# Attention feeding a spectral mix on one core: two pairs' row sums moved to the vector engine, one weight block split elsewhere, and a reordered vector queue in every sixth slot

## The chip, the cores and the metric

The kernel runs on one core of one Trainium2 chip. The metric is the device time of one execution in microseconds. Three runs of the kernel before took 980.04, 981.16 and 984.58 us; the median, 981.16, is what the changed kernel is compared with.

## What is computed

Attention with 8 batches, 12 heads, 448 positions and 64 channels per head, with scores capped by tanh, and behind it a mixing layer over the 768 channels that the heads make together:

```python
scores = scale * np.matmul(q, k.transpose(0, 1, 3, 2))
scores = cap * np.tanh(scores / cap)
scores = scores - np.max(scores, axis=-1, keepdims=True)
attn = np.exp(scores)
attn = attn / (np.sum(attn, axis=-1, keepdims=True) + 1e-09)
x = np.matmul(attn, v)              # then (batch, 448, 768)
theta = x @ w_theta
zr, zi = x * np.cos(theta), x * np.sin(theta)
y = einsum('ts,bsd->btd', w_tok_r, zr) + einsum('ts,bsd->btd', w_tok_i, zi)
u = x + y
out = u + np.maximum(u @ w_ch, 0.0)
```

All arrays are float32. Where the cap is at most 64 the kernel leaves out the subtraction of the maximum; that is the arm that runs here.

## The kernel before

**The unit of work is a pair of heads**, 48 in all (8 batches of 6 pairs), one pair `k` per slot `s`. A slot forms the scores of pair `s` in two halves (`qk_half`, L193), and on ScalarE tanh (L195) and exp (L201, `exp_half`) of each half; for the pair of the slot before it forms the product with v (`av`, L233; ScalarE copies it out, L236) and the row sums. Slots 0 to 7 are the start, in which the weights are loaded and split too. From slot 8 on every slot also carries one sixth of the mixing layer of one batch: slot `8 + 6b + part`, with `part` 0 to 5 and a script of its own for each part (`part_scripts`, L359). There are 56 slots.

**Row sums.** `sums` (L250) multiplies a matrix of ones with the exponentials and leaves them in a PSUM tile `r` for two pairs. Pairs below `DIRECT` feed their four chunks to TensorE (`sum_pair`, L239: 8 matmuls for a pair; the trace shows two records for each). The pairs from `DIRECT` on are first added up on VectorE to a tile `ps` (`add_half`, L215: one add at L223, two at L226), and both pairs of a sum go to TensorE together, with 2 matmuls each. `invert` (L265) takes the reciprocal of `r` on VectorE and sends it by four DMAs (L279) to the tiles `bc`; `norm` (L281) multiplies by them later.

**Matmuls of reduced precision in two parts.** The weights and, in the mixing layer, the data are split into a high and a low part. A weight block is loaded (`load`, L95), scaled (`scale`, L100, on ScalarE) and split (`split`, L103) by six or seven operations on VectorE: L106 to L109, then the cast to the high part, on ScalarE (L111) for `w_ch` and on VectorE (L113) for the others, then L114 and L115 for the low part. Where the cast is on ScalarE, ScalarE waits for L107, and VectorE for the cast. The blocks are called th0 to th5 (`w_theta`), ch0 to ch5 (`w_ch`) and tk0 to tk6 (`w_tok`). th and ch blocks are loaded into the two buffers `g_sb`, even ones into the first and odd ones into the second, which the mixing layer uses as well; tk blocks go through the buffers of the tiles `zh` and `zl`.

**When a weight step is done** stands in the table `WEIGHTS` (L142): for slot and place in it (`a`, `b`, `c`) a list of steps, `>x` for load, `*x` for scale, `x` for split. From pair 14 (`WHOLE`) on q and k are split as well: `prep` (L174) makes the tiles `hi` and `lo` of the next pair on VectorE (L178, L179) and issues the next load of q, k. DMAs are all issued from SP's queue, in the program's order, and a DMA that waits for its buffer holds up those behind it.

**The mixing layer of a batch.** Parts 0 and 1: six projections `th` (`theta`, L306; L299 to L301), brought to the range of the sine by ScalarE (L310, L311) and VectorE (L312 to L314); sines and cosines on ScalarE (`sincos`, three blocks at a time); `rotate` (L321) multiplies them with x on VectorE. From part 1's end to part 3: `transp` (L325) transposes a block on TensorE in two PSUM tiles of 4 and 3 pieces; for each ScalarE makes the high part `zh` (L333) and VectorE the low part `zl` (L334); `mix` (L337) multiplies them with the tk weights, and VectorE adds the result to x (L344). Parts 4 and 5: six projections `ch` (`chan`, L346), their result (L352) and the output.

**PSUM.** The scores take one tile in psS. All else, the results `a`, `r`, `th`, `t`, `mx` and `ch`, comes from one pool, psM, with four buffers. A new tile takes a buffer whose readers stand ahead of it in the program, the one that is freed first there, and its first matmul waits for that reader.

The engines run their own queues in the order in which the program is written; nothing is reordered.

Of the kernel before, what the change touches and what calls it, by code (L numbers as in the profile page):

```python
# [25 lines left out]

FIRST = 8

DIRECT = 10

WHOLE = 14

# [2 lines left out]
def softcap_attn_then_spectral_mix(ctx, tc, qk2, v, cap, w_theta, w_tok, w_ch, ident, outT):  # L35
    nc = tc.nc
# [7 lines left out]
    NS = B * NP  # L44
# [7 lines left out]
    w_theta, w_ch = (w.bitcast(I32).rearrange("m p j (n two) -> m p j n two", two=2) for w in (w_theta, w_ch))  # L52
# [16 lines left out]
    wch_h = const.tile([P, NJ, DM], F32R, name="wch_h")  # L69
    wch_l = const.tile([P, NJ, DM], F32R, name="wch_l")  # L70
# [14 lines left out]
    class Split:  # L85
# [14 lines left out]
        def scale(self):  # L100
            nc.scalar.activation(self.hw, self.hw, AF.Copy, scale=2.0**-112)

        def split(self):  # L103
            t, hi, lo, hw, lw = self.t, self.hi, self.lo, self.hw, self.lw
            ti = t.bitcast(I32)
            nc.vector.tensor_scalar(ti, hw.bitcast(I32), 3, None, op0=ALU.logical_shift_left)  # L106
            nc.vector.scalar_tensor_tensor(ti, hw.bitcast(I32), -(2**31), ti, op0=ALU.bitwise_and, op1=ALU.bitwise_or)  # L107
            nc.vector.tensor_scalar(hw.bitcast(I32), ti, -(2**23), None, op0=ALU.bitwise_and)
            nc.vector.scalar_tensor_tensor(lw, lw.bitcast(U32), 2.0**-52, hw, op0=ALU.mult, op1=ALU.mult)  # L109
            if self.act:  # L110
                nc.scalar.copy(hi, t)  # L111
            else:
                nc.vector.tensor_copy(hi, t)  # L113
            nc.vector.tensor_tensor(t, t, hi.bitcast(F32), op=ALU.subtract)  # L114
            nc.vector.tensor_tensor(lo, t, lw, op=ALU.add)  # L115

    def room_g(i):
        def room():
            st = g_sb[i % 2].rearrange("p x y s -> p (x y s)")
            raw = st[:, : 2 * DM].rearrange("p (j n two) -> p j n two", j=NJ, two=2)  # L120
            return raw, st[:, 2 * DM : 3 * DM].rearrange("p (j n) -> p j n", j=NJ)
        return room
# [8 lines left out]
    steps = {}  # L131

    def weight_steps():
        for m in range(NJ):
            ms = slice(m * P, (m + 1) * P)
            steps["th", m] = Split(room_g(m), w_theta[m], wth_h[:, :, ms], wth_l[:, :, ms])
            steps["ch", m] = Split(room_g(m), w_ch[m], wch_h[:, :, ms], wch_l[:, :, ms], True)
        for c in range(NC2):
            steps["tk", c] = Split(room_z(S, f"swk{c}"), w_tok[c], wtk_h[:, c], wtk_l[:, c])

# [7 lines left out]
    }  # L148

    def weights(s, pos):  # L150
        for word in WEIGHTS.get((s, pos), "").split():
            step = steps[word[-3:-1], int(word[-1])]
            {">": step.load, "*": step.scale}.get(word[0], step.split)()


    hi, lo, vt, pt, pst, bc = {}, {}, {}, {}, {}, {}
# [17 lines left out]
    def prep(k):  # L174

        hi[k] = wk.tile([P, 2, S], F32R, tag="hi", name=f"hi{k}", bufs=1)
        lo[k] = wk.tile([P, 2, S], F32R, tag="lo", name=f"lo{k}", bufs=1)
        nc.vector.tensor_copy(hi[k], raw[k])  # L178
        nc.vector.tensor_tensor(lo[k], raw[k], hi[k].bitcast(F32), op=ALU.subtract)  # L179
        if k + 1 < NS:  # L180
            load_qk(k + 1)
# [83 lines left out]
    def invert(k):  # L265

        if k % 2 == 0:
            return
        r = state.pop("r")
        ri = wk.tile([P, S], F32, tag="ri", name=f"ri{k}", bufs=1)  # L270
        if state["general"]:
            nc.vector.tensor_scalar_add(ri, r[:, :S], 1e-9)
            nc.vector.reciprocal(ri, ri)
        else:
            nc.vector.reciprocal(ri, r[:, :S])  # L275
        for n in (k - 1, k):
            bc[n] = wk.tile([P, S], F32, tag="bc", name=f"bc{n}", bufs=2)
            for i in range(2):
                nc.sync.dma_start(bc[n][i::2, :], ri[D * (n % 2) : D * (n % 2) + D, :])  # L279
# [90 lines left out]
    def us(b, j):  # L370
        split_x(b, j, "us")

    def pipeline(general):
        state["general"] = general
        load_v(0)
        load_qk(1)
        for step in (("tk", 0), ("tk", 1)):
            steps[step].load()

        for s in range(FIRST + 6 * B):  # L380
            k = s - 1
            b, part = divmod(s - FIRST, 6)
            live = s < NS
            start = s < FIRST
            if live:
                qk_half(s, 0)
            if start:
                weights(s, "a")
                exp_half(s, 0)
            if 0 <= k < NS:  # L390
                av(k)
            if not start:
                weights(s, "a")
            if not start and part == 4:
                for j in range(NJ // 2, NJ):
                    us(b, j)
            if s + 1 < NS:
                load_v(s + 1)
            if 0 <= k < NS:
                sums(k, (0,) if start else (0, 1))  # L400
                if not start:
                    invert(k)
            if live:
                qk_half(s, 1)
            if 0 <= k and start:
                sums(k, (1,))
            if s + 2 <= WHOLE:
                load_qk(s + 2)
            if WHOLE <= s + 1 < NS:
                prep(s + 1)  # L410
            weights(s, "b")
            if 0 <= k and start:
                invert(k)
            script = ["B", "a", "b"] if start else part_scripts(b)[part]
            for i, e in enumerate(script):
                if not start and i == len(script) - 1:
                    weights(s, "c")
                    if s % 2 == 1 and s <= NS + 1:
                        norm(s - 3)
                        norm(s - 2)  # L420
                if isinstance(e, str):
                    if live:
                        if e in "AB":
                            exp_half(s, "AB".index(e))
                        else:
                            add_half(s, "ab".index(e))
                else:
                    e[0](b, e[1])
            if start:
                weights(s, "c")  # L430
                for n in {4: (0, 1), 5: (2, 3), 7: (4, 5)}.get(s, ()):
                    norm(n)
                for j in {6: range(4), 7: range(4, NJ)}.get(s, ()):
                    split_x(0, j, "xs")
# [52 lines left out]
```

## Time and profile before

| | |
|---|---|
| median of 3 runs | 981.16 us (980.04 to 984.58) |
| profiled execution, its own time | 981.55 us |
| its span, first to last instruction | 979.7 us |
| granted clock of TensorE, mean of the span | 0.995 |
| TensorE busy | 953.9 us (97%) |
| VectorE busy | 631.6 us (64%) |
| ScalarE busy | 597.4 us (61%) |
| DMA queue of the program | 22.7% of 16 engines' span |

Busy times are of one profiled execution; 1.85 us of its time lie around the span. Times in the rows further on are microseconds from the span's start. On TensorE's timeline slot 9 begins at 107.9, slot 10 at 129.5, slot 11 at 154.5, slot 12 at 175.6, slot 13 at 194.2, and slot 16, the part 2 of batch 1, runs from 252.5 to 275.8. A matmul's duration in the profile overlaps that of its neighbours, so the cost of a train of matmuls is read from its start to the start of the next one. The granted clock is 1.00 at 2.4 GHz; 0.5 would be 1.2 GHz throughout.

### The profile page before, as it was taken

The page shows a single profiled execution, that of the slowest core. Times are in us where ns is not written, and L with a number is a line of the kernel's source. Part 1 is how long each engine was busy: PE and PEld are TensorE (multiplying, and loading weights), DVE is VectorE, ACT ScalarE, POOL GpSimd, SP SyncE. Part 2 cuts the span into 40 slices and gives each one's busy share as a digit, 9 for nine tenths or more (in the row PEclk, how much of TensorE's full clock was granted, in tenths as well). Part 3 has the DMA queues.
Part 4 walks back from the last instruction along what each step waited for, and adds up shares of the span by engine and source line. Part 5 has one row for each costly group of instructions (what it writes and reads, how often), then busy time and mean ns, then how long its engine had stood idle before and what let it go on. Part 6 is the DMA issues. An engine that isn't in the chain of part 4 may idle for free.

```text
span 979.7 us, 12717 instructions
## 1 busy us (share of the span) xinstructions
PE 953.9 (97%) x5192; PEld 693.5 (71%) x5192; DVE 631.6 (64%) x865; ACT 597.4 (61%) x615; POOL 0.4 (0%) x6
## 2 busy tenths in 40 slices
PE   6999999989999999999999999999999999999997
PEld 2333667657787787777677767876877777789897
DVE  5788665885865658557676567665586566763541
ACT  5887676466954677555876469636784567642520
POOL 0000000000000000000000000000000000000000
PEclk9999999999999999999999999999999999999999
DMA  6654221322102211032111321122211330102001
GB/s 221 196 186 127 66 69 39 121 98 85 48 29 76 79 54 48 30 104 76 38 48 36 106 67 46 49 68 75 66 48 29 86 93 29 29 1 76 1 1 60
DMA packets 30739, 68.68 MB, mean 70 GB/s; under 512 B 4304, under 2 KB 16720, under 8 KB 30672
## 3 DMA queue, kind: packets, MB, share of 16 engines
q1 hardware_dynamic: 30672, 67.78, 22.7%
q8 instruction: 43, 0.70, 0.3%
q14 instruction: 24, 0.20, 0.1%
HBM read 45.74 MB, written 11.01 MB: 58 GB/s over the span
## 4 chain that ended last, share of the span: by engine, by line
PE 78%; DVE 10%; ACT 9%; DMA 2%; issue 1%; SPq 0%; DVEq 0%
PE a L233 13%; PE s L193 12%; PE mx L341 6%; PE mx L342 6%; PE mx L343 6%; PE ch L299 6%; PE ch L301 6%; PE ch L300 6%; PE th L299 4%; PE th L300 4%; PE th L301 4%; PE r L248 3%; ACT p L195 3%; PE t L332 3%; DVE ri L275 2%; ACT p L201 1%
## 5 line engine op out<-in xcount | busy, mean ns | idle before, releaser
L195 ACT ACTIVATE p<-s,qscale 112x1792 f32<-112x1792 f32 x96 | 168.7, 1757 | 171.2 <-PE s L193 171.1
L201 ACT ACTIVATE p<-p,cap_sb 112x1792 f32<-112x1792 f32 x96 | 170.6, 1790 | 0.5
L233 PE MATMUL a<-p,v 112*64 112x448 f32 x768 | 155.5, 547 | 0.0
L341 PE MATMUL mx<-wtk_h,zh 128*128 128x448 f32 x336 | 126.3, 376 | 1.8 <-DVE zl L334 1.8
L342 PE MATMUL mx<-wtk_l,zh 128*128 128x448 f32 x336 | 122.9, 366 | 0.0
L343 PE MATMUL mx<-wtk_h,zl 128*128 128x448 f32 x336 | 122.9, 366 | 0.0
L233 PEld LDWEIGHTS a<-p,v 112*64 112x64 f32 x768 | 51.0, 137 | 87.9 <-issue 78.5
L299 PE MATMUL ch<-us,wch_h 128*128 128x448 f32 x288 | 107.2, 372 | 0.0
L299 PE MATMUL th<-xs,wth_h 128*128 128x448 f32 x288 | 106.9, 371 | 0.0
L301 PE MATMUL ch<-us,wch_l 128*128 128x448 f32 x288 | 105.6, 367 | 0.0
L300 PE MATMUL ch<-us,wch_h 128*128 128x448 f32 x288 | 105.5, 366 | 0.0
L300 PE MATMUL th<-xs,wth_h 128*128 128x448 f32 x288 | 105.4, 366 | 0.0
L301 PE MATMUL th<-xs,wth_l 128*128 128x448 f32 x288 | 105.3, 366 | 0.0
L226 DVE TENSOR_TENSOR ps<-ps,p 112x896 f32<-112x896 f32 x76 | 82.7, 1088 | 1.3
L275 DVE RECIPROCAL ri<-r 128x448 f32<-128x448 f32 x24 | 70.9, 2954 | 14.8 <-PE r L248 14.8
L312 DVE SCALAR_TENSOR_TENSOR g_sb<-g_sb 128x448 f32<-128x448 f32 x48 | 30.0, 624 | 72.6 <-ACT g_sb L311 72.2
L334 DVE TENSOR_TENSOR zl<-t,zh 128x512 fp32r<-128x512 f32 x96 | 55.2, 617 | 24.9 <-ACT zh L333 24.9
L341 PEld LDWEIGHTS mx<-wtk_h,zh 128*128 128x128 f32 x336 | 63.2, 188 | 7.7 <-DVE zl L334 3.0
L352 DVE SCALAR_TENSOR_TENSOR x<-ch,x 128x448 f32<-128x448 f32 x48 | 29.8, 621 | 59.0 <-PE ch L301 59.0
L343 PEld LDWEIGHTS mx<-wtk_h,zl 128*128 128x128 f32 x336 | 63.1, 188 | 5.3
L342 PEld LDWEIGHTS mx<-wtk_l,zh 128*128 128x128 f32 x336 | 63.2, 188 | 4.8
L344 DVE TENSOR_TENSOR x<-mx,x 128x448 f32<-128x448 f32 x48 | 29.9, 623 | 52.9 <-PE mx L343 52.3
(71 smaller groups left out, 1411.6 us busy)
## 6 DMA issues: line engine op xcount, KB each, us to landing
qk_sb<-in_qk SPq DMA_DIRECT2D x35, 448.0 KB, 3.3
v<-in_v SPq DMA_DIRECT2D x48, 224.0 KB, 2.5
bc<-ri SPq DMA_DIRECT2D x96, 112.0 KB, 2.3
out_dram<-x SPq DMA_DIRECT2D x48, 224.0 KB, 2.0
qk<-in_qk SPq DMA_DIRECT2D x13, 448.0 KB, 3.3
g_sb<-in_wth SPq DMA_DIRECT2D x6, 768.0 KB, 5.1
g_sb<-in_wch SPq DMA_DIRECT2D x6, 768.0 KB, 5.3
swk_raw<-in_wtok SPq DMA_DIRECT2D x7, 448.0 KB, 4.2
```

The lines of the kernel that those rows point to most:

```text
L193: nc.tensor.matmul(sp[:CP, i, hh, :S], kk[k][rows, 1, ks], qq[k][rows, 0, :], start=n == 0, stop=n == len(products) - 1)
L195: nc.scalar.activation(pp, sp[:CP, :, :, :S], AF.Tanh, scale=qscale[:CP])
L201: nc.scalar.activation(pp, pp, AF.Exp, scale=cap_sb[:CP])
L226: nc.vector.tensor_tensor(pst[k], pst[k], pt[k, 1][:, i], op=ALU.add)
L233: nc.tensor.matmul(acc[hh * D : (hh + 1) * D, :S], va[:, hh, c, :], pt[k, c // 2][:, c % 2, hh, :], start=c == 0, stop=c == NCH - 1)
L275: nc.vector.reciprocal(ri, r[:, :S])
L299: nc.tensor.matmul(acc[:, :S], wh[:, j, ms], t[:, 0, :], start=j == 0, stop=False)
L300: nc.tensor.matmul(acc[:, :S], wh[:, j, ms], t[:, 1, :], start=False, stop=False)
L301: nc.tensor.matmul(acc[:, :S], wl[:, j, ms], t[:, 0, :], start=False, stop=j == NJ - 1)
L341: nc.tensor.matmul(acc[:, :S], zh[:, c, :], wtk_h[:, c, :], start=c == 0, stop=False)
L342: nc.tensor.matmul(acc[:, :S], zh[:, c, :], wtk_l[:, c, :], start=False, stop=False)
L343: nc.tensor.matmul(acc[:, :S], zl[:, c, :], wtk_h[:, c, :], start=False, stop=c == NC2 - 1)
```

## The change

- Pairs 8 and 9 are no longer direct: their exponentials are added on VectorE in slots 8 and 9, and their row sums go to TensorE together in slot 10.
- The split of tk6 moves from the end of slot 8 to the start of slot 9, ahead of that of ch1.
- Block ch2 is scaled on VectorE (`vscale`) and cast to its high part on VectorE, at the start of slot 11, where it was scaled before on ScalarE; its split stood at the end of that slot. The load of ch4 follows that split, and the load of ch3 alone stays at the end of slot 11.
- In slots of part 2 the reciprocal with its DMAs, and the split of q, k of the next pair with its load, stand behind the first step of the script, `transp` of block 1 with its casts and its low part; they stood ahead of the script.

```diff
--- before.py
+++ after.py
@@ -26,7 +26,7 @@
 
 FIRST = 8
 
-DIRECT = 10
+DIRECT = 8
 
 WHOLE = 14
 
@@ -99,6 +99,9 @@
 
         def scale(self):
             nc.scalar.activation(self.hw, self.hw, AF.Copy, scale=2.0**-112)
+
+        def vscale(self):
+            nc.vector.tensor_scalar_mul(self.hw, self.hw, 2.0**-112)
 
         def split(self):
             t, hi, lo, hw, lw = self.t, self.hi, self.lo, self.hw, self.lw
@@ -134,7 +137,7 @@
         for m in range(NJ):
             ms = slice(m * P, (m + 1) * P)
             steps["th", m] = Split(room_g(m), w_theta[m], wth_h[:, :, ms], wth_l[:, :, ms])
-            steps["ch", m] = Split(room_g(m), w_ch[m], wch_h[:, :, ms], wch_l[:, :, ms], True)
+            steps["ch", m] = Split(room_g(m), w_ch[m], wch_h[:, :, ms], wch_l[:, :, ms], m != 2)
         for c in range(NC2):
             steps["tk", c] = Split(room_z(S, f"swk{c}"), w_tok[c], wtk_h[:, c], wtk_l[:, c])
 
@@ -144,13 +147,14 @@
         (2, "a"): "*th2", (2, "b"): "th2 >th4", (2, "c"): "*tk1", (3, "a"): "*th3", (3, "b"): "tk1 >tk3 th3 >th5",
         (3, "c"): "*tk2", (4, "a"): "*th4", (4, "b"): "th4 >ch0", (4, "c"): "*tk3", (5, "b"): "tk2 >tk4 tk3 >tk5",
         (5, "c"): "*th5", (6, "b"): "th5 >ch1", (6, "c"): "*tk4", (7, "a"): "*ch0", (7, "b"): "tk4 >tk6 ch0", (7, "c"): "*tk5",
-        (8, "b"): "tk5", (8, "c"): "*tk6 tk6 *ch1", (9, "a"): "ch1", (10, "c"): ">ch2", (11, "a"): "*ch2", (11, "c"): "ch2 >ch4 >ch3", (12, "b"): "*ch3 ch3 >ch5", (12, "c"): "*ch4 ch4", (13, "b"): "*ch5 ch5",
+        (8, "b"): "tk5", (8, "c"): "*tk6 *ch1", (9, "a"): "tk6 ch1", (10, "c"): ">ch2", (11, "a"): "#ch2 ch2 >ch4",
+        (11, "c"): ">ch3", (12, "b"): "*ch3 ch3 >ch5", (12, "c"): "*ch4 ch4", (13, "b"): "*ch5 ch5",
     }
 
     def weights(s, pos):
         for word in WEIGHTS.get((s, pos), "").split():
             step = steps[word[-3:-1], int(word[-1])]
-            {">": step.load, "*": step.scale}.get(word[0], step.split)()
+            {">": step.load, "*": step.scale, "#": step.vscale}.get(word[0], step.split)()
 
 
     hi, lo, vt, pt, pst, bc = {}, {}, {}, {}, {}, {}
@@ -398,7 +402,7 @@
                 load_v(s + 1)
             if 0 <= k < NS:
                 sums(k, (0,) if start else (0, 1))
-                if not start:
+                if not start and part != 2:
                     invert(k)
             if live:
                 qk_half(s, 1)
@@ -406,7 +410,7 @@
                 sums(k, (1,))
             if s + 2 <= WHOLE:
                 load_qk(s + 2)
-            if WHOLE <= s + 1 < NS:
+            if WHOLE <= s + 1 < NS and (start or part != 2):
                 prep(s + 1)
             weights(s, "b")
             if 0 <= k and start:
@@ -426,6 +430,11 @@
                             add_half(s, "ab".index(e))
                 else:
                     e[0](b, e[1])
+                if part == 2 and i == 0 and not start:
+                    if 0 <= k < NS:
+                        invert(k)
+                    if WHOLE <= s + 1 < NS:
+                        prep(s + 1)
             if start:
                 weights(s, "c")
                 for n in {4: (0, 1), 5: (2, 3), 7: (4, 5)}.get(s, ()):
```

Lines of the changed kernel stand 3 or 4 further down than those of the kernel before (L275 is now L279, L334 is L338, L312 is L316, L106 is L109).

VectorE in slot 16 (part 2 of batch 1), before: from rotate of block 2 to rotate of block 3. `ri` is the reciprocal, `hi` and `lo` are q, k of pair 17, `zl_1` is the low part of block 1.

```order
L323 TENSOR_TENSOR g_sb_86<-g_sb_86,x_734 128x896
L275 RECIPROCAL ri_1770<-r_1765 128x448
L178 CAST hi_1793<-qk_sb 128x896
L179 TENSOR_TENSOR lo_1794<-qk_sb,hi_1793 128x896
L334 TENSOR_TENSOR zl_1_1799<-t_1_0_1800,zh_1_1798 128x512
L334 TENSOR_TENSOR zl_1_1799<-t_1_4_1807,zh_1_1798 128x384
L344 TENSOR_TENSOR x_534<-mx_0_1815,x_534 128x448
L323 TENSOR_TENSOR g_sb_87<-g_sb_87,x_875 128x896
```

The same place in the changed kernel:

```order
L327 TENSOR_TENSOR g_sb_86<-g_sb_86,x_731 128x896
L338 TENSOR_TENSOR zl_1_1782<-t_1_0_1783,zh_1_1781 128x512
L338 TENSOR_TENSOR zl_1_1782<-t_1_4_1790,zh_1_1781 128x384
L279 RECIPROCAL ri_1796<-r_1761 128x448
L182 CAST hi_1804<-qk_sb 128x896
L183 TENSOR_TENSOR lo_1805<-qk_sb,hi_1804 128x896
L348 TENSOR_TENSOR x_534<-mx_0_1811,x_534 128x448
L327 TENSOR_TENSOR g_sb_87<-g_sb_87,x_874 128x896
```

The two operations on `zl_1` now stand ahead of the reciprocal, the `hi` and the `lo`.

SP's queue from slot 10 to the end of slot 11, before: `bc` are the copies of 1/sums, `g_sb_86` the first weight buffer (ch2, then ch4), `g_sb_87` the second (ch3).

```order
L279 DMA bc_889<-ri_887 64x448 x2
L279 DMA bc_892<-ri_887 64x448 x2
L168 DMA qk_902<-in_qk 128x896
L97 DMA g_sb_86<-in_wch 128x1536
L172 DMA v_1049<-in_v 112x512
L168 DMA qk_1058<-in_qk 128x896
L97 DMA g_sb_86<-in_wch 128x1536
L97 DMA g_sb_87<-in_wch 128x1536
```

The same in the changed kernel (one more row ahead, the load of v 11):

```order
L176 DMA v_876<-in_v 112x512
L172 DMA qk_890<-in_qk 128x896
L283 DMA bc_909<-ri_907 64x448 x2
L283 DMA bc_912<-ri_907 64x448 x2
L97 DMA g_sb_86<-in_wch 128x1536 x2
L176 DMA v_1053<-in_v 112x512
L172 DMA qk_1062<-in_qk 128x896
L97 DMA g_sb_87<-in_wch 128x1536
```

The load of q, k 12 is ahead of the copies; the load of ch4 follows directly on that of ch2, ahead of those of v 12 and q, k 13; ch3's is still last.

VectorE from theta 1 in slot 8 to the split of ch1 in slot 9, before: `swk` is the buffer of tk6, `g_sb_86` in 448 columns the theta blocks, `g_sb_87` in 768 columns ch1.

```order
L314 TENSOR_SCALAR g_sb_86<-g_sb_86 128x448
L106 TENSOR_SCALAR swk_t<-swk_raw 128x448
L107 SCALAR_TENSOR_TENSOR swk_t<-swk_raw,swk_t 128x448
L108 TENSOR_SCALAR swk_raw<-swk_t 128x448
L109 SCALAR_TENSOR_TENSOR swk_raw<-swk_raw 128x448
L113 CAST wtk_h<-swk_t 128x448
L114 TENSOR_TENSOR swk_t<-swk_t,wtk_h 128x448
L115 TENSOR_TENSOR wtk_l<-swk_t,swk_raw 128x448
L312 SCALAR_TENSOR_TENSOR g_sb_86<-g_sb_86 128x448
L313 TENSOR_SCALAR g_sb_86<-g_sb_86 128x448
L314 TENSOR_SCALAR g_sb_86<-g_sb_86 128x448
L106 TENSOR_SCALAR g_sb_87<-g_sb_87 128x768
```

The same in the changed kernel, from the last adds of pair 8:

```order
L230 TENSOR_TENSOR ps_660<-ps_660,p_1_620 112x896 x2
L316 SCALAR_TENSOR_TENSOR g_sb_86<-g_sb_86 128x448
L317 TENSOR_SCALAR g_sb_86<-g_sb_86 128x448
L318 TENSOR_SCALAR g_sb_86<-g_sb_86 128x448
L109 TENSOR_SCALAR swk_t<-swk_raw 128x448
L110 SCALAR_TENSOR_TENSOR swk_t<-swk_raw,swk_t 128x448
L111 TENSOR_SCALAR swk_raw<-swk_t 128x448
L112 SCALAR_TENSOR_TENSOR swk_raw<-swk_raw 128x448
L116 CAST wtk_h<-swk_t 128x448
L117 TENSOR_TENSOR swk_t<-swk_t,wtk_h 128x448
L118 TENSOR_TENSOR wtk_l<-swk_t,swk_raw 128x448
L109 TENSOR_SCALAR g_sb_87<-g_sb_87 128x768
```

The theta block (three rows) now stands ahead of the seven rows of tk6, and the adds of pair 8 ahead of both; the split of ch1 follows directly on that of tk6.

## Rows read from the trace of the kernel before

**Rows 1.** Page, busy time of the engines: us, share of the span, instructions.

```profile
PE 953.9 (97%) x5192; PEld 693.5 (71%) x5192; DVE 631.6 (64%) x865; ACT 597.4 (61%) x615; POOL 0.4 (0%) x6
```

**Rows 2.** TensorE's waits: who waited for whom, us in total, times, longest.

```profile
PE s L193 <- ACT p L195: 8.9, 10, 2.8
PE t L332 <- DVE zl L334: 4.6, 6, 0.8
```

**Rows 3.** Timeline of TensorE, slots 10 and 12: start, us, operation, records, [idle before].

```profile
134.38 3.20 PE L248 MATMUL r<-p,ones_sb 112*32 112x448 f32 x16
137.52 1.76 PE L193 MATMUL s<-qk 64*112 64x448 f32 x8
...
180.42 0.96 PE L248 MATMUL r<-ps,ones_sb 112*32 112x448 f32 x8
181.31 1.76 PE L193 MATMUL s<-qk 64*112 64x448 f32 x8
```

**Rows 4.** Page, costliest groups: busy us, mean ns of one, idle before.

```profile
L226 DVE TENSOR_TENSOR ps<-ps,p 112x896 f32<-112x896 f32 x76 | 82.7, 1088 | 1.3
```

**Rows 5.** Timelines of ScalarE, VectorE and TensorE at the end of slot 9.

```profile
117.68 1.76 ACT L195 ACTIVATE p<-s,qscale 112x1792 f32<-112x1792 f32 x1 [3.29 <-PE s L193]
...
125.85 1.08 DVE L323 TENSOR_TENSOR g_sb<-g_sb,x 128x896 f32<-128x896 f32 x1
...
128.68 0.93 PE L332 MATMUL t<-ident_sb,g_sb 128*128 128x128 f32 x7
```

**Rows 6.** Timelines of VectorE and SP, slot 11.

```profile
165.09 1.16 DVE L334 TENSOR_TENSOR zl<-t,zh 128x512 fp32r<-128x512 f32 x2 [6.74 <-ACT zh L333]
...
175.13 0.55 DVE L106 TENSOR_SCALAR g_sb<-g_sb 128x768 int32<-128x768 int32 x1
...
180.05 1.16 DVE L283 TENSOR_TENSOR x<-bc,x 128x448 f32<-128x448 f32 x2
...
180.17 0.80 SPq L97 DMA_DIRECT2D g_sb<-in_wch  x2
```

**Rows 7.** Timelines of VectorE and ScalarE, slots 12 and 13.

```profile
183.26 2.95 DVE L275 RECIPROCAL ri<-r 128x448 f32<-128x448 f32 x1
188.72 0.56 DVE L106 TENSOR_SCALAR g_sb<-g_sb 128x768 int32<-128x768 int32 x1 [2.50 <-ACT g_sb L101]
...
187.78 0.91 ACT L101 ACTIVATE g_sb<-g_sb 128x768 f32<-128x768 f32 x1 [2.84 <-DMA g_sb<-in_wch]
...
199.41 0.83 ACT L111 CAST wch_h<-g_sb 128x768 fp32r<-128x768 f32 x1 [4.08 <-DVE g_sb L107]
```

**Rows 8.** Timeline of TensorE, slot 13.

```profile
201.95 2.61 PE L193 MATMUL s<-qk 64*112 64x448 f32 x8 [2.83 <-ACT p L195]
```

**Rows 9.** Stretches: length, busy us of PE, PEld, DVE, ACT, POOL, granted clock, DMA, GB/s.

```profile
202.00:204.50 2.50, 2.50 (x9) 0.74 (x9) 1.90 (x3) 0.32 (x1) 0.00 (x0) 0.65 0.10 38
204.50:208.00 3.50, 3.50 (x16) 3.18 (x15) 1.82 (x3) 2.55 (x2) 0.00 (x0) 0.76 0.67 188
...
265.00:267.00 2.00, 1.23 (x8) 1.00 (x8) 2.00 (x5) 1.98 (x4) 0.00 (x0) 1.00 0.79 177
```

**Rows 10.** Timeline of TensorE, slot 16.

```profile
264.43 0.60 PE L332 MATMUL t<-ident_sb,g_sb 128*128 128x128 f32 x4
...
266.26 0.48 PE L341 MATMUL mx<-wtk_h,zh 128*128 128x448 f32 x1
...
270.65 0.93 PE L332 MATMUL t<-ident_sb,g_sb 128*128 128x128 f32 x7
271.33 0.45 PE L341 MATMUL mx<-wtk_h,zh 128*128 128x448 f32 x1
```

**Rows 11.** Timelines of VectorE and ScalarE, slot 16.

```profile
260.58 2.95 DVE L275 RECIPROCAL ri<-r 128x448 f32<-128x448 f32 x1
...
261.09 0.95 ACT L333 CAST zh<-t 128x512 fp32r<-128x512 f32 x2
```

## Prediction

> **What bounds the kernel now.** I read the busy time of the engines first, then TensorE's waits, then the timeline of the slots that the change touches. TensorE is busy 97% of the span; no other engine comes near it [rows 1]. So a term counts only if it takes work off TensorE, or shortens a wait in front of it. Of its waits two belong to edited places [rows 2]: 8.9 us behind ScalarE's tanh, of which 2.83 is one wait in slot 13 [rows 8], and 4.6 us behind VectorE's low part `zl`, in six part-2 slots, 0.77 each. The rest of the 8.9 lies in the first slots, which the change leaves alone.
>
> **Term 1, the row sums of pairs 8 and 9.** Today each pair feeds its four chunks to TensorE: a train of 16 records (two for each of 8 instructions) from 134.38 to the next start at 137.52, 3.14 us; the train of slot 9 is the same. With the adds on VectorE one train of 8 records in slot 10 serves both pairs, as in slot 12: 180.42 to 181.31, 0.89 us [rows 3]. TensorE loses 2 x 3.14 - 0.89 = **5.4 us** of work. VectorE gains six adds of 1.09 [rows 4], 3.3 us in slot 8 and as much in slot 9. What covers them there: VectorE waits for ScalarE between the theta groups. The split of tk6 moves behind them, and so the split of ch1 comes later; its second operation releases ScalarE's cast of ch1, and behind that cast stand tanh of slot 9, the sines, the reduction of theta 3 and then VectorE's rotate of block 0.
>
> That chain is late next. Today tanh starts at 117.68 as soon as TensorE has its scores (ScalarE waited 3.29 for it), the rotate ends at 125.85 + 1.08 = 126.93, and the first transposes start at 128.68, 1.75 later [rows 5]. TensorE will be there 3.14 earlier, at 125.54. If ScalarE comes no earlier than today, TensorE waits 1.4; if it follows TensorE fully, 0. The cast in front of tanh lets it come about 1 us earlier by my count of the queue, nearer to the first end: I take **+0.5** (0 to 1.4). In slot 10 the sum matmuls of pair 9 wait for its last add, which stands two theta groups behind exp: **+0.2** (0 to 0.5).
>
> **Term 2, ch2 early.** Today ch2 is split at the end of slot 11; only then are the loads of ch4 and ch3 issued, at 180.17 [rows 6]. ScalarE waits 2.84 for ch3's load (to 187.78), VectorE behind it 2.50 (to 188.72), and VectorE's work then runs on without a gap to the split of ch4, whose second operation releases ScalarE's cast at 199.41 after 4.08 of waiting [rows 7]. Behind that cast stands tanh of slot 13, and behind tanh TensorE with its 2.83 us wait at 201.95 [rows 8]. In the change ch2 goes through scale and split at the start of slot 11 on VectorE. Its six operations took 175.13 to 180.05, 4.9 us; the cast to the high part and the scale come to VectorE too. Each is a pass with one source, as the first of the block with 0.55 [rows 6]; the scale is not in the trace, and I bound it by 0.55 and by 1.09, an add with two sources [rows 4], and take 0.55. Together 6.0 us. They are hidden, because VectorE idles 6.74 there today, up to 165.09 [rows 6]; if that cover failed, the low part of block 4 would be late by the overhang.
>
> So the split ends at 165.09 - 6.74 + 6.0 = 164.4 on today's clock, and the load of ch4 leaves then, 15.8 earlier than today. On the SP queue it waits for that split with the loads of v 12, q, k 13 and ch3 behind it. Today's pair of loads took 187.78 - 180.17 = 7.6 to land; from some 166 on that is 174, and ch3 is wanted at 184.9, the others later still: nothing. Also moved are q, k 12 ahead of the four copies of 1/sums (nobody waits) and ch2's load behind them: it must land before slot 11, some 5 us later; covered. ScalarE loses a scale and a cast that it had time for: nothing.
>
> With ch3 loaded, ScalarE's scale starts at 187.78 - 2.84 = 184.94, and VectorE is free after its reciprocal at 183.26 + 2.95 = 186.2 [rows 7] instead of 188.72. The whole chain comes 2.5 earlier, the exps between the two casts too. Of the 2.83 wait 0.33 stays. The wait also costs clock: after it the granted clock is 0.65 over 2.5 us and 0.76 over 3.5 us, a mixture of 1.2 and 2.4 GHz; at 2.4 the same work takes 2.5 x 0.35 + 3.5 x 0.24 = 1.7 us less. After the 0.77 us wait in slot 16 it is 1.00 [rows 9], so a remaining 0.33 should not lower it. Term 2: 2.5 + 1.7 = **4.2 us** (2.5 if the clock falls all the same, 4.5 if the wait goes altogether).
>
> **Term 3, part-2 slots.** Today VectorE does the reciprocal (and the split of q, k) ahead of `zl` of block 1. The four psM buffers go to the next tiles in the order in which their readers stand: the second half of block 2's transposes gets what `zl` frees, and waits. The pair of tiles and the mix behind it start at 264.43 and 266.26, 1.83 apart; undisturbed it is 271.33 - 270.65 = 0.68 [rows 10]. Lost: 1.15 per slot, not 0.77 alone. In the change `zl` stands first: both halves of block 2 find their buffers, but mix 1 gets the buffer of r, and **waits for the reciprocal**, a wait that replaces the old one. When does that end? VectorE is free at 260.58, where the reciprocal starts today. ScalarE's cast pair starts at 261.09 and takes 0.95 [rows 11], so `zl` begins at about 261.7, its two halves take 1.1 (the pair of rows 6), and the reciprocal runs from 262.8 to 265.7. Mix 1 could start at 264.43 + 0.68 = 265.1: it waits 0.65. Gain 0.5 per slot, six slots: **3.0 us** (0 to 6.9). Split of q, k, mix add and rotate 3 follow some 2 us later than today, but are wanted only at the next transposes (270) and the next slot (276). Slot 10 has no wait today, since it splits no q, k; there the new one comes on top: **+0.65**.
>
> **The sum:** 5.4 + 4.2 + 3.0 - 0.65 - 0.5 - 0.2 = 11.25 us. The profiled execution took 981.55, the median of the runs is 981.16, 0.4 less; I go by the median: 969.9, say **970.0 us**.
>
> **Rivals.**
> A, the reciprocal ends later than I reckon and mix 1 waits as long as is lost today: term 3 is nothing, 973.0. For: `zl` waits for a cast, so VectorE stands idle 1 us that it does not today. Against: the distances of rows 10 and 11.
> B, the change doesn't cure slot 13: ch3's load, now behind ch4's wait on SP, or ch4's cast still comes late. Without term 2: 974.2. For: one queue, four transfers behind one wait. Against: over 10 us of slack.
> C, mix 1 gets another buffer and waits for nothing: term 3 is 6 x 1.15 = 6.9 and slot 10 costs nothing: 965.4. Against: the order of readers.
> D, the seven new waits cost clock. If it falls at each as in slot 13, 7 x 1.7 = 11.9 are lost: 981.9, no change. Against: clock 1.00 after 0.77 us [rows 9]. The Trainium skill, in "TensorE: Matmul & The Clock Gate", section "A second HAM failure mode: psum-queue depth-cycling", says that cycling through PSUM buffers can leave TensorE idle in small pieces so often that its clock swings between half and full. By that rule D would come about; at this very place the trace does not agree, with its 1.00.
> E, slower: in part-2 slots VectorE falls so far behind ScalarE's cast that mix 1 waits as TensorE did in slot 13, 2.83 and 1.7 for the clock. Then 7 x 4.53 = 31.7 are paid, 6.9 saved there, and 5.4 + 4.2 - 0.7 = 8.9 elsewhere: 981.2 + 15.9 = 997. Without loss of clock it decides from a wait of (6.9 + 8.9) / 7 = 2.3 us on. For: the reciprocal takes 2.95 by itself. Against: the cast would have to come 1.6 later than in rows 11, and nothing ahead of it is moved.
>
> **Chances and range.** A measurement of this kernel tells about 0.5% from no change, 4.9 us: faster is below 976.3. Forecast 0.68, A 0.09, B 0.09, C 0.06, D 0.05, E 0.03. Faster takes the first four: 0.92; the same is D, 0.05; slower is E, 0.03. The forecast's own range is 967.5 to 972.5, from the bounds of slots 9 and 10 and of term 3. The range takes in A and B and an unlucky end of slot 9 with either, and stops short of C, D and E: 966 to 975.
>
> **What would show it.** Right: TensorE's row sums fed from `p` are 8 trains of 16 records; TensorE's wait in slot 13 is under 0.5 us with the clock at 1.00 behind it; no wait for `zl` in front of transposes, in its place seven waits of mix 1 for the reciprocal, about 0.65 each; a wait of about 0.5 for the rotate in slot 9. Wrong: a long wait for tanh still in slot 13 (B), mix 1 waiting over 1 us (A, E), a clock below 1.00 in part-2 slots (D), or VectorE's low part of block 4 late behind ch2.

## The result and the profile after

The changed kernel took 971.51 us (median of 5 runs, 969.56 to 975.09), the kernel before 981.26 beside it (5 runs): ratio 0.990, 95% interval 0.988 to 0.993. The forecast was 970.0, between 966 and 975. The medians differ by 9.75, where 11.25 was forecast. The profiled execution took 970.66 us, its span is 968.9 where that before was 979.7. The busy times [rows 1] are now:

```profile
PE 947.1 (98%) x5168; PEld 691.3 (71%) x5168; DVE 638.8 (66%) x873; ACT 595.3 (61%) x613; POOL 0.4 (0%) x6
```

TensorE is busy 6.8 us less. What it waits for, in the view of rows 2:

```profile
PE s L197 <- ACT p L199: 5.6, 9, 1.9
...
PE mx L345 <- DVE ri L279: 3.6, 7, 0.5
...
PE t L336 <- DVE g_sb L327: 0.3, 1, 0.3
```

The waits for `zl` in front of transposes are gone; in their place stand seven of the mix for the reciprocal `ri`, and there is one new wait for the rotate. The long wait of slot 13 is no longer among those for `p`. TensorE's timeline at these places (rows 3, 5, 8 and 10 of before):

```profile
125.59 0.96 PE L336 MATMUL t<-ident_sb,g_sb 128*128 128x128 f32 x7 [0.27 <-DVE g_sb L327]
...
131.33 1.39 PE L252 MATMUL r<-ps,ones_sb 112*32 112x448 f32 x8
132.65 1.76 PE L197 MATMUL s<-qk 64*112 64x448 f32 x8
...
139.44 0.93 PE L336 MATMUL t<-ident_sb,g_sb 128*128 128x128 f32 x7
140.88 0.44 PE L345 MATMUL mx<-wtk_h,zh 128*128 128x448 f32 x1 [0.52 <-DVE ri L279]
...
195.09 1.76 PE L197 MATMUL s<-qk 64*112 64x448 f32 x8
...
256.05 0.93 PE L336 MATMUL t<-ident_sb,g_sb 128*128 128x128 f32 x7
257.48 0.44 PE L345 MATMUL mx<-wtk_h,zh 128*128 128x448 f32 x1 [0.51 <-DVE ri L279]
```

One train of sums, eight records, stands where two of sixteen stood; it starts 1.32 before the next scores, not 0.89. The second train of scores of slot 13, at 195.09, has no listed wait. Mix 1 starts 1.44 and 1.43 after the transposes; undisturbed that is 0.68 [rows 10], so the wait listed as 0.51 costs 0.75 from start to start.

**Where the time went, slot by slot.** I read the start of the first train of scores of a slot in each trace and subtract. The last column runs to the last train of scores (slot 47). "Start" is the time at which the second train of scores of slot 1 begins; from there to slot 9 every execution takes 85.3 to 85.4 us.

| us | start | slot 9 | slot 10 | slot 11 | slots 12, 13 | slot 14 to 47 | from slot 9 |
|---|---|---|---|---|---|---|---|
| before | 22.55 | 21.65 | 24.95 | 21.08 | 40.87 | 639.42 | 747.97 |
| after | 22.15 | 18.98 | 23.89 | 21.06 | 36.62 | 637.02 | 737.57 |
| difference | -0.40 | -2.67 | -1.06 | -0.02 | -4.25 | -2.40 | -10.40 |
| forecast | | -2.64 | -1.40 | 0 | -4.2 | -3.0 | -11.25 |

The 0.40 in front is no part of the change; with it the two spans differ by 10.8. The first trains of scores take between 1.76 and 3.33 us, differently from execution to execution:

```profile
15.66 3.33 PE L193 MATMUL s<-qk 64*112 64x448 f32 x8 [1.85 <-ACT p L195]
```

is the third train in one experiment (part 2 alone, below; its start is 24.98), and

```profile
14.52 1.76 PE L196 MATMUL s<-qk 64*112 64x448 f32 x8 [2.34 <-ACT p L198]
```

in another (ch2 alone; start 20.99). Over the 13 executions profiled the start lies between 20.99 and 25.47. Behind the last train of scores they take 123.8 to 123.9 us, and 125.4 in two (only ch3's load; the change without ch2), where the clock fell behind a wait that all 13 have (last section). The start is thus the larger part of what the columns leave out. The other executions left no trace, so that their times differ for the same reason is not shown. The experiments are read by the columns from slot 9 on, one profiled execution each, with the medians beside them.

### The profile page after: what moved, and what is told of

The parts are those of the page before. It is cut to its first block, busy times and chain, and to the rows that moved or that the text cites. A ratio compares the mean times of both kernels' runs of the same rounds, so it can differ in the third digit from the quotient of the medians.

```text
span 968.9 us, 12676 instructions
## 1 busy us (share of the span) xinstructions
PE 947.1 (98%) x5168; PEld 691.3 (71%) x5168; DVE 638.8 (66%) x873; ACT 595.3 (61%) x613; POOL 0.4 (0%) x6
## 4 chain that ended last, share of the span: by engine, by line
PE 88%; DVE 5%; ACT 5%; issue 1%; DMA 0%; SPq 0%
PE a L237 15%; PE s L197 14%; PE mx L345 6%; PE mx L346 6%; PE mx L347 6%; PE th L303 6%; PE ch L303 6%; PE ch L305 6%; PE th L304 6%; PE ch L304 6%; PE th L305 6%; PE r L252 3%; ACT p L199 3%; PE t L336 3%; DVE ri L279 2%
## 5 line engine op out<-in xcount | busy, mean ns | idle before, releaser
L230 DVE TENSOR_TENSOR ps<-ps,p 112x896 f32<-112x896 f32 x80 | 87.0, 1087 | 1.4
L279 DVE RECIPROCAL ri<-r 128x448 f32<-128x448 f32 x24 | 70.8, 2952 | 12.5 <-PE r L252 12.4
L316 DVE SCALAR_TENSOR_TENSOR g_sb<-g_sb 128x448 f32<-128x448 f32 x48 | 30.0, 624 | 66.4 <-ACT g_sb L315 66.0
L338 DVE TENSOR_TENSOR zl<-t,zh 128x512 fp32r<-128x512 f32 x96 | 55.2, 616 | 24.5 <-ACT zh L337 24.5
L303 PEld LDWEIGHTS ch<-us,wch_h 128*128 128x128 f32 x288 | 54.1, 188 | 9.7 <-issue 4.6
```

The lines of the kernel that those rows point to most:

```text
L230: nc.vector.tensor_tensor(pst[k], pst[k], pt[k, 1][:, i], op=ALU.add)
L303: nc.tensor.matmul(acc[:, :S], wh[:, j, ms], t[:, 0, :], start=j == 0, stop=False)
```

## Experiments

**The sums alone.**

```diff
-DIRECT = 10
+DIRECT = 8
```

> The kernel before with the row sums of pairs 8 and 9 added on VectorE, and nothing else (the split of tk6 stays at the end of slot 8). Theory (term 1 stands by itself): TensorE's train of 16 records fed from p is gone from slots 9 and 10, 2 x 3.14 - 0.89 = 5.4 us less, and 0.3 to 0.9 us come back as waits for the last add and for rotate; 976.4 to 977.0 where the kernel before takes 981.3. The wait of 2.8 us in slot 13 stays as it is. Rival (the slots behind are set by VectorE and DMA, so time saved ahead of them becomes waiting): the wait in slot 13 grows by what is saved, 980 to 981.3.

974.14 us (before 981.64; ratio 0.992, 0.991 to 0.993), less than the theory's 976.4 to 977.0. From slot 9 on it is 7.16 less: 2.83 in slot 9 and 1.74 in slot 10, 4.57 together as the theory has it, and a further 2.63 in slots 12 and 13, which neither the theory nor the rival had:

```profile
175.56 0.80 SPq L97 DMA_DIRECT2D g_sb<-in_wch  x2
```

SP's issue of the loads of ch4 and ch3, then ScalarE and TensorE:

```profile
182.06 0.91 ACT L101 ACTIVATE g_sb<-g_sb 128x768 f32<-128x768 f32 x1 [1.73 <-DMA g_sb<-in_wch]
```

```profile
196.24 1.76 PE L193 MATMUL s<-qk 64*112 64x448 f32 x8 [1.72 <-ACT p L195]
```

and the stretch behind that wait (columns of rows 9):

```profile
196.20:198.70 2.50, 2.46 (x12) 1.36 (x13) 2.41 (x4) 1.00 (x2) 0.00 (x0) 1.00 0.07 27
```

The loads reach ScalarE 6.50 after their issue, before 7.61 [rows 6, 7]; the wait is 1.72 instead of 2.83 [rows 8], and the clock stays at 1.00 where it was 0.65. So the terms are not independent: with the sums moved, a good half of term 2 comes without ch2 being touched. Here tk6 is still split at the end of slot 8, and slot 9 takes 18.82; in the changed kernel, with tk6 moved, it takes 18.98. Moving the split of tk6 to slot 9 gained nothing there.

**ch2 alone.** Of the table WEIGHTS the diffs show the entries that differ.

```diff
+        def vscale(self):
+            nc.vector.tensor_scalar_mul(self.hw, self.hw, 2.0**-112)
...
-            steps["ch", m] = Split(room_g(m), w_ch[m], wch_h[:, :, ms], wch_l[:, :, ms], True)
+            steps["ch", m] = Split(room_g(m), w_ch[m], wch_h[:, :, ms], wch_l[:, :, ms], m != 2)
...
-        (11, "a"): "*ch2", (11, "c"): "ch2 >ch4 >ch3",
+        (11, "a"): "#ch2 ch2 >ch4", (11, "c"): ">ch3",
...
-            {">": step.load, "*": step.scale}.get(word[0], step.split)()
+            {">": step.load, "*": step.scale, "#": step.vscale}.get(word[0], step.split)()
```

> The kernel before with block ch2 alone scaled and split on VectorE at the start of slot 11, with the load of ch4 behind it and that of ch3 alone at the slot's end. Theory (term 2 stands by itself): the wait for tanh in slot 13 falls from 2.83 to at most 0.4 us, and the granted clock behind it stays at 1.00; 4.2 to 4.5 us less, 976.8 to 977.1 where the kernel before takes 981.3. Rival B (the load of ch3, behind that of ch4 on SP, or the cast of ch4 still comes late): the wait stays above 2 us, 980.5 to 981.3. Rival (the clock falls although the wait is short): 978.8.

978.97 (ratio 0.997, 0.996 to 0.998): 2.7 less by the medians, 4.21 by the columns from slot 9, of it 4.25 in slots 12 and 13 (36.62). No wait of slot 13 is listed. The median misses the theory's 976.8 to 977.1 and lies at the second rival's 978.8, and the profiled execution, with the earliest start of all, is the fastest of eleven (975.88 to 981.35). Against that rival, a clock that falls behind a short wait, speak all eight traces in which the load of ch3 does not stand behind a late split of ch2: slots 12 and 13 take 36.6 to 36.7 in each. Why the median gained less than the trace is not shown; the start may be the reason.

**Part 2 alone.**

```diff
-                if not start:
+                if not start and part != 2:
...
-            if WHOLE <= s + 1 < NS:
+            if WHOLE <= s + 1 < NS and (start or part != 2):
...
+                if part == 2 and i == 0 and not start:
+                    if 0 <= k < NS:
+                        invert(k)
+                    if WHOLE <= s + 1 < NS:
+                        prep(s + 1)
```

> The kernel before with the reciprocal and the split of q, k behind the first transposes of block 1 in slots of part 2, and nothing else. Theory (term 3 stands by itself, sized by the trace of the changed kernel, where a batch takes 0.40 us less than before): 6 x 0.40 gained and 0.75 lost in slot 10, 1.65 us less, 979.6 where the kernel before takes 981.3; seven waits of mix for the reciprocal of about 0.5 us, none for zl. Rival A (the new waits cost what the old ones did): 981.3 to 982. Rival D (the new waits cost clock): over 985, with a granted clock below 1.00 in these slots.

981.34 (ratio 0.9995, 0.9985 to 1.0004): no change that the medians can tell, and not the theory's 979.6. By the columns of the one trace 1.83 less: 2.44 from slot 14 on, 6 x 0.41, and 0.77 lost in slot 10; the rest lies in slots 11 to 13. The waits are those expected:

```profile
PE mx L341 <- DVE ri L275: 3.6, 7, 0.5
```

Rival D is out: it expected over 985. The median lies in rival A's range; the columns speak for the theory.

**Only ch3's load.**

```diff
-(11, "c"): "ch2 >ch4 >ch3"
+(11, "c"): ">ch3 ch2 >ch4"
```

> The kernel before with one change: at the end of slot 11 the load of ch3 is issued ahead of the split of ch2 instead of behind the load of ch4; ch2 stays on ScalarE and at the end of the slot. Theory (slot 13's wait comes from the late load of ch3 alone): ScalarE's scale of ch3 waits for no DMA, VectorE's split of ch3 starts 2.5 us earlier, the wait in slot 13 falls from 2.83 to at most 0.4 us with the clock at 1.00; 976.8 to 977.1 where the kernel before takes 981.3. Rival (it is the five us of ch2's split that VectorE has to get rid of, or the load of ch4 becomes the late one): the wait stays above 1.5 us, 979.5 to 981.3.

979.10 (ratio 0.996, 0.995 to 0.998), again above the theory's range by the median; slots 12 and 13 take 36.72, 4.15 less, in an execution that is the slowest of its eleven (981.83; start 25.47). ch2 is still split at the slot's end. On SP two loads stand in one row: ch3's leaves at once, ch4's waits for that split, to the row's end at 183.4:

```profile
164.79 18.61 SPq L97 DMA_DIRECT2D g_sb<-in_wch  x2
```

ScalarE's scale of ch3, and TensorE in slot 13:

```profile
187.74 0.91 ACT L101 ACTIVATE g_sb<-g_sb 128x768 f32<-128x768 f32 x1
```

```profile
202.21 1.76 PE L193 MATMUL s<-qk 64*112 64x448 f32 x8 [0.18 <-ACT p L195]
```

The scale has no wait for a DMA, and TensorE waits 0.18 where it waited 2.83. That settles the cause of the wait: ch3's late load. Moving ch2 to VectorE was one way to it, and not a needed one.

**The change without ch2, and the sums once more.** Both ask whether the earlier landing belongs to the moved sums or was chance.

```diff
-ms], m != 2)
+ms], True)
...
-(11, "a"): "#ch2 ch2 >ch4", (11, "c"): ">ch3"
+(11, "a"): "*ch2", (11, "c"): "ch2 >ch4 >ch3"
```

> The changed kernel with the part on ch2 undone: ch2 scaled on ScalarE and split at the end of slot 11, the loads of ch4 and ch3 behind that split. Theory 1 (the term of ch2 stands by itself whatever the other terms do): the wait in slot 13 is 2.8 us again and the clock falls behind it; slots 12 and 13 take 40.9 us instead of 36.6, 976.2 where the changed kernel takes 972.0. Theory 2 (with the sums moved, the loads of ch4 and ch3 land some 1 us sooner after their issue, as in the run with the sums alone, where the wait was 1.72 and the clock stayed at 1.00): slots 12 and 13 take 38.2 us, 973.6. Which of the two it is depends on the time from the issue of the two loads to ScalarE's scale of ch3: 7.5 to 7.6 us by theory 1, 6.5 by theory 2.

972.96 (before 981.24; ratio 0.992, 0.990 to 0.993). Issue to scale 6.42 us, wait 1.63, slots 12 and 13 38.16.

> The run with the sums alone once more, on another chip perhaps. Theory 2 (the earlier landing belongs to this program): the loads of ch4 and ch3 reach ScalarE 6.5 us after their issue, the wait in slot 13 is 1.7 us, the clock stays at 1.00; 974.1. Theory 1 (it was chance): 7.5 us, a wait of 2.8, 976.8.

974.31 (ratio 0.993, 0.992 to 0.994). Issue to scale is 6.51 again, so the earlier landing goes with the moved sums, as far as five traces tell: 6.42 to 6.51 in three with the sums moved and ch2 left, 7.50 (part 2 alone) and 7.61 in the two without. In all five the issue stands 25.7 us behind the start of slot 11, with the same load of v behind it, so it is not the place of the issue in its slot. Why the load lands 1.1 us sooner there is open. But the clock of the profiled execution, the slowest of the six (978.40), fell behind the same wait, and slots 12 and 13 took 39.81:

```profile
198.79 3.05 PE L193 MATMUL s<-qk 64*112 64x448 f32 x8 [1.73 <-ACT p L195]
```

```profile
198.80:201.30 2.50, 2.50 (x8) 0.91 (x8) 1.94 (x3) 0.36 (x1) 0.00 (x0) 0.56 0.09 35
```

A wait of 1.72 left the clock at 1.00 in one execution, one of 1.73 took it to 0.56 in another of the same program. What ch2's part gives on top of the others is thus 38.16 - 36.62 = 1.5 us, and 3.2 where the clock falls (39.81 - 36.62).

**The reciprocal later still.**

```diff
                 if part == 2 and i == 0 and not start:
-                    if 0 <= k < NS:
-                        invert(k)
                     if WHOLE <= s + 1 < NS:
                         prep(s + 1)
+                    if 0 <= k < NS:
+                        invert(k)
```

> The changed kernel with the split of q, k ahead of the reciprocal behind the first transposes in slots of part 2, so that the reciprocal ends 1.66 us later in six of the seven slots (in slot 10 no q, k is split). Theory (the wait is paid one for one, and the clock does not fall at waits of about 2 us with work close around them): 6 x 1.66 = 10 us more than the changed kernel, 981.5 where that takes 971.5, clock 1.00. Rival (a wait of 2 us costs clock as the one of 2.83 in slot 13 did, 1.7 us each): 991.7, with a granted clock of 0.65 to 0.8 behind each wait. Rival (the time comes back elsewhere in the slot): under 975.

983.88 (ratio to before 1.003, 1.002 to 1.004), and 972.00 for the changed kernel on the same chip: 11.9 more, between the two. TensorE's waits for `ri`, and the stretches behind the first three long ones:

```profile
PE mx L345 <- DVE ri L279: 13.6, 7, 2.2
```

```profile
258.80:260.80 2.00, 2.00 (x6) 1.80 (x7) 2.00 (x4) 1.99 (x2) 0.00 (x0) 0.51 0.44 99
...
376.70:378.70 2.00, 2.00 (x10) 1.85 (x11) 2.00 (x4) 1.99 (x2) 0.00 (x0) 1.00 0.36 84
...
493.00:495.00 2.00, 1.98 (x8) 1.85 (x9) 2.00 (x4) 1.99 (x2) 0.00 (x0) 0.84 0.43 96
495.00:498.00 3.00, 3.00 (x10) 2.66 (x9) 0.42 (x1) 0.44 (x1) 0.00 (x0) 0.54 0.39 89
```

All six waits from slot 16 on are 2.17 long (the one in slot 10 is 0.52); behind two the clock fell, behind four it stayed at 1.00. From slot 14 on the kernel takes 13.0 more: 6 x 1.66 = 10.0 for the waits, and 3.0 for two falls, 1.5 each, near the 1.7 that the prediction took from rows 9.

**The changed kernel again.**

> The changed kernel again, beside its own variants: 971.5, within the spread of its runs (969.6 to 975.1).

972.00 (before 981.45 on this chip; ratio 0.991, 0.989 to 0.992); 737.66 from slot 9 on, 737.57 the first time.

**The reciprocal ahead, only the split of q, k behind.** On VectorE the order is now reciprocal, `zl`, `hi` and `lo`.

```diff
-                if not start and part != 2:
+                if not start:
                     invert(k)
...
                 if part == 2 and i == 0 and not start:
-                    if 0 <= k < NS:
-                        invert(k)
```

> The changed kernel with the reciprocal and its DMAs back ahead of the script in slots of part 2; only the split of q, k stays behind the first transposes. Theory (one buffer of psM goes to mix 1 from whichever reader on VectorE stands last, and it is the reciprocal's 2.95 us in front of it that make it wait): the reciprocal ends at about 263.5 on the clock of the kernel before, the two operations on zl by 264.6, and mix 1, wanted at 265.1, waits for nothing: 7 x 0.75 = 5.2 us less than the changed kernel, 966.3 where that takes 971.5. Rival (zl is wanted earlier than I reckon, or the cast pair is late): the second half of block 2's transposes waits for zl again, 0.2 us or more; 968 to 971.5.

966.00 (ratio to before 0.984, 0.983 to 0.986), 6.0 less than the changed kernel beside it. From slot 14 on 4.61 less, 6 x 0.77, and 0.68 in slot 10. Its trace lists no wait for `ri` at all. In slot 16 VectorE does:

```profile
252.03 2.95 DVE L279 RECIPROCAL ri<-r 128x448 f32<-128x448 f32 x1
254.90 1.09 DVE L338 TENSOR_TENSOR zl<-t,zh 128x512 fp32r<-128x512 f32 x2
```

The reciprocal starts in the time in which VectorE idled 1.04 in the changed kernel (below). By the order of readers the low part, 1.1 us long, is now what frees the buffer of mix 1; that is argued, no view shows which buffer a tile gets. What the run shows: without the split of q, k between the reciprocal and `zl` the old wait is gone as well, and no new one comes. So in the kernel before it was that split which cost time.

**ch1 ahead of tk6.**

On top of the edit before:

```diff
-(9, "a"): "tk6 ch1"
+(9, "a"): "ch1 tk6"
```

> As the run with the reciprocal back ahead of the script, and ch1 split ahead of tk6 at the start of slot 9. Theory (the cast of ch1 stands ahead of tanh of slot 9, so it is tk6's 3 us ahead of it that make rotate late): the wait for rotate of 0.27 us in slot 9 goes, and some of the 0.43 us by which the sums of slot 10 wait; 0.3 to 0.7 us less than that run. Rival (tk6's split is late next, for mix 0 of slot 10, or nothing moves): the same within 0.2 us, or a new wait in front of mix 0.

965.07 (ratio to before 0.983, 0.982 to 0.985). Slot 9 takes 18.53 instead of 18.97, slot 10 22.71 instead of 23.21, 0.94 in all, a little more than expected. The wait for the rotate is gone, and no other is listed in its place. The train of sums in slot 10 is undisturbed again, 0.89 to the next scores:

```profile
131.47 0.96 PE L252 MATMUL r<-ps,ones_sb 112*32 112x448 f32 x8
132.36 1.76 PE L197 MATMUL s<-qk 64*112 64x448 f32 x8
```

**The same, with ch2 as before and only ch3's load first.**

```diff
-ms], m != 2)
+ms], True)
...
-(11, "a"): "#ch2 ch2 >ch4", (11, "c"): ">ch3"
+(11, "a"): "*ch2", (11, "c"): ">ch3 ch2 >ch4"
```

> The version with the reciprocal ahead of the script and ch1 ahead of tk6, and ch2 as in the kernel before (scale on ScalarE, split at the end of slot 11), but with the load of ch3 ahead of that split. Theory (only the time at which ch3 is loaded matters): the wait in slot 13 is at most 0.3 us, and the time that of the version with ch2 on VectorE, 965.1 within 0.5. Rival (VectorE needs the five us at the end of slot 11 when TensorE is this much earlier, or the load of ch4 is late): over 966.5.

965.12 (before 981.24; ratio 0.984, 0.982 to 0.985); slots 12 and 13 take 36.70 with a wait of 0.18. So this version needs no new code for ch2. It and the two before it beat both the kernel before and the changed kernel.

## Why the prediction was right, step by step

**Term 1, the row sums: right in slot 9, 0.23 too good in slot 10.** Slot 9 gives 2.67 where 3.14 - 0.5 was reckoned. The late rotate is the cause of what is missing: the version that splits ch1 ahead of tk6 has no such wait, and there slot 9 gives 3.12. The count behind the 0.5 holds too. The rotate ends 17.94 behind the start of slot 9, where it ended at 19.04 (126.93 - 107.89) before, 1.10 sooner:

```profile
124.36 1.08 DVE L327 TENSOR_TENSOR g_sb<-g_sb,x 128x896 f32<-128x896 f32 x1
```

In slot 10 the sums wait for the last add by 1.32 - 0.89 = 0.43, taken as 0.2 within 0 to 0.5; the bound was right, the choice within it low.

**Term 2, ch2 early: 4.25 of 4.2, but the step "ch2 early" named a wider cause than there is.** The chain came as told: ch2 on VectorE ends at 160.3, as reckoned (164.4 with slot 11 starting 4.1 earlier), and the low part of block 4 still has 0.64 of cover,

```profile
159.38 0.96 DVE L118 TENSOR_TENSOR wch_l<-g_sb 128x768 fp32r<-128x768 f32 x1
...
160.98 1.15 DVE L338 TENSOR_TENSOR zl<-t,zh 128x512 fp32r<-128x512 f32 x2 [0.64 <-ACT zh L337]
```

SP holds the load of ch4 for that split, with the three loads behind it, and is done in good time,

```profile
143.26 17.43 SPq L97 DMA_DIRECT2D g_sb<-in_wch  x2
...
161.74 0.37 SPq L97 DMA_DIRECT2D g_sb<-in_wch  x1
```

ScalarE finds ch3 loaded, and tanh of slot 13 comes early enough that the clock behind it stays up (0.65 in rows 9):

```profile
180.69 0.91 ACT L101 ACTIVATE g_sb<-g_sb 128x768 f32<-128x768 f32 x1
```

```profile
195.00:197.50 2.50, 2.41 (x12) 1.31 (x13) 2.40 (x4) 1.11 (x3) 0.00 (x0) 1.00 0.04 16
...
257.40:259.40 2.00, 1.92 (x10) 1.81 (x11) 1.97 (x4) 1.98 (x4) 0.00 (x0) 1.00 0.38 85
```

Rival B did not come about; the slack on SP was there. That the size fits to 0.05 is in part luck, since two errors of 0.2 cancel. From the first to the second train of scores slot 13 takes 5.02, before 7.74: 2.72 for the wait, where 2.5 was reckoned and 0.33 was to stay. From there to slot 14 it takes 1.53 less, which is what the clock gave back, where 1.7 was reckoned. What the prediction did not see is that the sums alone shorten the same wait. The sum still holds, because the wait can only go once: 7.16 + 4.21 + 1.83 = 13.2 for the three parts alone, 10.40 together.

**Term 3, part 2: the mechanism right, 2.40 instead of 3.0.** The operations stand where they were reckoned. Slot 16 starts at 244.07, 8.38 earlier than before (252.45), and the reckoned 261.7 and 262.8 become 253.32 and 254.42:

```profile
253.32 1.16 DVE L338 TENSOR_TENSOR zl<-t,zh 128x512 fp32r<-128x512 f32 x2 [1.04 <-ACT zh L337]
254.39 2.95 DVE L279 RECIPROCAL ri<-r 128x448 f32<-128x448 f32 x1
```

The step that was mis-sized is "it waits 0.65": the reciprocal ends at 257.34, and mix 1 starts at 257.48. This 0.14 between the end of the releasing operation and the start of the released one was left out. Undisturbed, mix 1 would start at 256.05 + 0.68 = 256.73; from there it is 0.61 to the end of the reciprocal, and with the 0.14 it is 0.75. Against 0.65 that is 0.1 in each of six slots and in slot 10: 0.7 us of the 0.85 by which the forecast was too good. The other 0.23 is slot 10's wait for the add, less small differences.

**The rivals.** A (mix 1 waits as long as is lost today) is refuted by the 0.75 against 1.15. C (no wait) did not come about in the change, but it is what the version with the reciprocal ahead does: 966.0, reckoned 965.4. D (the clock) did not come about: it is 1.00 behind all seven new waits, as in the row of 257.40 above. The Trainium skill, "TensorE: Matmul & The Clock Gate", section "A second HAM failure mode: psum-queue depth-cycling", has the clock swing where TensorE often idles for moments between groups of matmuls while it cycles through PSUM; at the seven waits of 0.5 us this trace does not agree, with its 1.00. These waits stand about 115 us apart, so what often repeated ones would do no run here shows. Behind the waits of 2.17 the clock fell in two of six. E needed waits over 2.3 us; waits of 2.17, brought about in the experiment, took the kernel to 983.88, 0.3% above the kernel before.

## What to carry to other kernels

Two edits that shorten the same wait don't add up: reckon each alone and both together, and ask of a wait which single transfer or operation ends it last, since moving that one may do (here one load, ahead of a split of 5 us). Where buffers are handed on in the order of their readers, the order of a vector queue decides which later tile waits: look for the order in which the long operation fills an idle stretch and a short one frees the buffer that is wanted first. Price a wait from start to start, and not by the idle time that is listed. Where a wait is reckoned from the end of its releaser, add what passes until the waiter starts: in these traces 0.15 us behind the reciprocal and the rotate, 0.06 behind the low part.

## What had not been expected of the hardware

The granted clock after a wait is not settled by the wait's length: 1.72 and 1.73 us in the same place gave 1.00 and 0.56, and of six waits of 2.17 two were followed by a fall. The last batch of every version has a wait of mix for `zl` of 1.82 or 1.83 us, about 56 us ahead of the end. Behind it the clock stayed at 1.00 in eleven of the 13 traces and fell in two, which then took 1.6 us longer. First the wait and the stretch behind it in the run with only ch3's load, then the stretch in the kernel before:

```profile
922.33 0.47 PE L341 MATMUL mx<-wtk_h,zh 128*128 128x448 f32 x1 [1.83 <-DVE zl L334]
```

```profile
922.30:924.80 2.50, 2.47 (x8) 2.26 (x9) 2.50 (x4) 2.11 (x2) 0.00 (x0) 0.66 0.00 0
```

```profile
923.50:926.00 2.50, 2.46 (x12) 2.29 (x13) 2.50 (x4) 2.13 (x2) 0.00 (x0) 1.00 0.00 0
```

What decides it no run here shows.

The first trains of scores take 1.76 to 3.33 us from execution to execution and move the second train of slot 1 by up to 4.5 us, more than most edits of this study bring. A train of this shape took 3.05 where the clock read 0.56 (the sums once more, slot 13), so 3.33 looks like a lower clock; but the granted clock reads 1.00 over 5 to 25 us in both of the executions quoted above, and why they differ is open.

And where the loads of ch4 and ch3 stand behind the late split of ch2, ScalarE's scale, which waits for ch3's load, starts 6.4 to 6.5 us after their issue with the sums moved and 7.5 to 7.6 without; the cause stays open.
